# A linear-attention and two-FFN kernel whose later eight head pairs project q and k from raw float32 values on 64-row halves

## The chip, the cores and the metric

The kernel runs on one core of a Trainium2 chip. The metric is the device time of one execution in microseconds. Before the change it is 931.89 us, the median of three runs (930.95 to 933.46).

The engines are TensorE (PE, with its weight loads shown as PEld), VectorE (DVE), ScalarE (ACT), GpSimd (POOL) and SyncE (SP, which issues most transfers).

## The reference

Attention over 4 batches of 8 heads, 576 positions, 64 values each, then two FFNs over the 2304 tokens. The change lies in phi, the first lines:

```python
def phi(x):
    proj = np.einsum('bhsd,df->bhsf', x, w_phi)            # 64 -> 128 features
    proj = proj - np.max(np.abs(proj), axis=-1, keepdims=True)
    return np.concatenate([np.exp(proj), np.exp(-proj)], axis=-1)
q_p, k_p = phi(q), phi(k)
kv = np.einsum('bhsf,bhsd->bhfd', k_p, v)
z = np.sum(k_p, axis=2)
num = np.einsum('bhsf,bhfd->bhsd', q_p, kv)
den = np.einsum('bhsf,bhf->bhs', q_p, z)[..., None] + 1e-06
attn = num / den
# tokens x 512:
h = x @ w_in;  x = np.maximum(0.01 * h, h) @ w_out         # first FFN, 2048 wide
h = x @ w_in2; out = (h / (1 + np.exp(-h))) @ w_out2       # second FFN
```

## The kernel before

**Pairs.** The 32 heads are worked on in 16 pairs. A pair's q and k lie transposed in SBUF, head 0 in rows 0 to 63 and head 1 in rows 64 to 127. So a projection has a contraction of 64 per head. k has 576 positions: four chunks of 128, and a tail of 64 per head that is packed into one product.

**Two forms of a projection.** The first eight pairs (`NFULL = 8`) multiply raw float32 values. Pairs 2 to 7 take `wraw`, phi's weights twice above each other, and give each head a product of its own on its 64 rows (`f_pk`, line 432, `f_pq`, line 462; the tail is `f_kt`, line 438). The later eight pairs work with a split: ACT copies a value into the float32r type (the high part), DVE subtracts to get the low part (`s_split`, lines 276 to 292), and PE multiplies the parts as float32r on all 128 rows. For k, `s_pk` has three products per chunk (high by high, low by high, high by low, lines 322 to 324) against a block-diagonal weight of 256 columns, so both heads come out of one product; two chunks share a PSUM bank. For q, `s_pq` puts high and low part of one head above each other in the 128 rows and has two products per head (lines 354 and 355). The tail has two (lines 335 and 336). The weights' own split, `WH`, `BDH` and `BDL`, is made once at the start (`split_consts`).

**After the projection** of a later pair: `k_sub` (lines 299 and 300, DVE) takes the largest magnitude and subtracts it, `k_exp` (308 and 309, ACT) makes both exponentials, `s_kv` the products with v (389, 394). For q, ACT copies the projection out of PSUM (357), POOL reduces it, `s_eq` makes the exponentials, `num_split` has twelve products per half of the positions (577) and two ACT copies per head (580, 581), and `s_fin` puts the result into the FFN's input. Each pair calls `s_pq` and `num_split` twice, for 288 positions each.

**What PE does between.** The later pairs run between the products of the first FFN: a step is twelve products into one bank (853) and twelve into four banks of the other tag (884). PSUM has eight banks: four under the tag `a`, shared by the projections, numerators and line 853, and four under `y`.

**What sets the order.** Up to a planned time of 150, tables (`ORDER`, `PLAN`, `SLOTS`, `EARLY`) give each step a time, and `in_order` and `pin` hold each engine to that order. The later pairs are placed by offsets (`OFF1`, one pair per eight units) among the FFN steps, and the framework's scheduler sets the order of the instructions on each engine from there, waiting for a PSUM bank or a buffer where it must.

Of the kernel before, what the change touches and what calls it, by code (L numbers as in the profile page):

```python
# [8 lines left out]
F32 = mybir.dt.float32  # L9
F32R = mybir.dt.float32r  # L10
U32 = mybir.dt.uint32
AF = mybir.ActivationFunctionType
# [90 lines left out]
EARLY = {  # L103
    (8, "lq"): (117.29,),
    (8, "lv"): (117.39,),
    (8, "sp"): (123.8, 127.98, 131.89, 133.51, 137.47, 140.31, 142.48, 147.66),
    (9, "lq"): (151.8,),
    (8, "pq0"): (161.92, 162.63),
    (8, "eq0"): (165.65, 167.79, 171.38, 172.55, 173.81),
# [12 lines left out]
def tile_linear_attention_ffn_ffn(ctx: ExitStack, tc: tile.TileContext, q, k, v, w_phi, w_in1, w_out1, w_in2, w_out2, out):  # L122


    nc = tc.nc
    B, H, S, D = 4, 8, 576, 64
    F = (w_phi.shape[1] - 128) // 3
# [5 lines left out]
    S0 = 512  # L133
# [3 lines left out]
    NFULL = 8  # L137
# [12 lines left out]
    attc = att_ctx.enter_context(tc.tile_pool(name="attc", bufs=1))  # L150
# [4 lines left out]
    def at(shape, dt, tag):  # L155
        return att_pool[0].tile(shape, dt, tag=tag, bufs=AB[0].get(tag, 1), name=tag)

    def ps(tag):

        return psp.tile([128, 512], F32, tag=tag, name=f"ps_{tag}")  # L160
# [3 lines left out]
    ring, WIDE = [0], 2  # L164
# [45 lines left out]
                last[ins.engine] = ins  # L210
        return last

    wc = at([128, 3 * F + 128], F32, "wc")
    BDF, wraw, ident = wc[:, 0 : 2 * F].rearrange("p (j f) -> p j f", j=2), wc[:, 2 * F : 3 * F], wc[:, 3 * F :]
    WH = attc.tile([128, F], F32R, name="WH")
    BDH = attc.tile([128, 2, F], F32R, name="BDH")
    BDL = attc.tile([128, 2, F], F32R, name="BDL")

    def make_consts():
        for c in (slice(0, 2 * F), slice(2 * F, 3 * F + 128)):  # L220
# [1 line left out]
        first = [const.tile([128, 2], F32, name=f"first{i}") for i in range(2)]  # L222
        nc.gpsimd.memset(first[0], 0.0)
        nc.gpsimd.partition_all_reduce(first[1], first[0], 128, bass_isa.ReduceOp.absmax)

    def split_consts():
        nc.scalar.activation(WH, wraw, AF.Copy)
        nc.scalar.activation(BDH, BDF, AF.Copy)
        nc.vector.tensor_sub(BDL, BDF, BDH.bitcast(F32))


    tiles1 = [(462 * i, 462) for i in range(2)] + [(924 + 460 * i, 460) for i in range(3)]
    X1 = {}
# [16 lines left out]
    P = [dict() for _ in range(B * HP)]  # L250
# [19 lines left out]
    def sub(out_, x, h):  # L270
        return nc.vector.tensor_tensor(out_, x, h.bitcast(F32), op=ALU.subtract)  # L271
# [1 line left out]
    def full(i):  # L273
        return i < NFULL

    def s_split(i):

        st = P[i]
        h, l = at([128, S0], F32R, "krh"), at([128, S0], F32R, "krl")
        nc.scalar.activation(h, st["kr"], AF.Copy)  # L280
        sub(l, st["kr"], h)
        st["krh"], st["krl"] = h, l
        qs = at([128, 2, S], F32R, "qs")
        for j in range(2):
            r, o = (slice(0, 64), slice(64, 128))[:: 1 - 2 * j]
            nc.scalar.activation(qs[r, j], st["qr"][r], AF.Copy)
            sub(qs[o, j], st["qr"][r], qs[r, j])
        st["qs"] = qs
        t = at([128, 128], F32R, "kth")
        nc.scalar.activation(t, st["kt"], AF.Copy)  # L290
        sub(t[64:128], st["kt"][64:128], t[64:128])
        st["kth"] = t

    def k_sub(i, pk, ng, g0):

        ke = P[i]["ke"]
        km = at([128, 4], F32, "km")
        src = pk[:, 0 : ng * F].rearrange("p (g f) -> p g f", f=F)
        nc.vector.tensor_reduce(km[:, 0:ng], src, op=ALU.max, axis=AX.X, apply_absolute_value=True)
        nc.vector.tensor_tensor(  # L300
            ke[:, g0 : g0 + ng, 0, :], src, km[:, 0:ng].unsqueeze(2).to_broadcast([128, ng, F]), op=ALU.subtract
        )
# [5 lines left out]
        nc.scalar.activation(e1, e0, AF.Exp, scale=-1.0)  # L308
        nc.scalar.activation(e0, e0, AF.Exp)

    def s_pk(c2):
        def f(i):
            st = P[i]
            if c2 == 0:
                st["ke"] = at([128, 9, 2, F], F32, "ke")
            pk = ps("a")
            for u in range(2):
                c = 2 * c2 + u
                cs = slice(c * 128, (c + 1) * 128)
                o = pk[:, u * 2 * F : (u + 1) * 2 * F]  # L320
                bh, bl = BDH.rearrange("p j f -> p (j f)"), BDL.rearrange("p j f -> p (j f)")
                nc.tensor.matmul(o, st["krh"][:, cs], bh, start=True, stop=False)
                nc.tensor.matmul(o, st["krl"][:, cs], bh, start=False, stop=False)
                nc.tensor.matmul(o, st["krh"][:, cs], bl, start=False, stop=True)
            k_sub(i, pk, 4, 4 * c2)
            if c2 == 0:
                k_exp(i, 0, 4)

        return f

    def s_pkt(i):
        st = P[i]
        pk = ps("a")
        o = pk[:, 0:F]
        nc.tensor.matmul(o, st["kth"], WH, start=True, stop=False)
        nc.tensor.matmul(o, st["kth"], BDL[:, 0], start=False, stop=True)
        k_sub(i, pk, 1, 8)
        k_exp(i, 4, 9)

    def part(i, a):  # L340
# [3 lines left out]
    def s_pq(a):  # L344

        def f(i):
            st = P[i]
            c0, n = part(i, a)
            p = at([128, 2 * n], F32, "p")
            st["p", a] = p  # L350
            pq = [ps("a"), ps("a")]
            cs = slice(c0, c0 + n)
            for j in range(2):
                nc.tensor.matmul(pq[j][:, 0:n], WH, st["qs"][:, j, cs], start=True, stop=False)  # L354
                nc.tensor.matmul(pq[j][:, 0:n], BDL[:, j], st["qs"][:, j, cs], start=False, stop=True)  # L355
            for j in range(2):
                nc.scalar.activation(p[:, j * n : (j + 1) * n], pq[j][:, 0:n], AF.Copy)  # L357
            m = at([128, 2 * n], F32, "m")
            nc.gpsimd.partition_all_reduce(m, p, 128, bass_isa.ReduceOp.absmax)  # L359
            st["m", a] = m  # L360

        return f

    def s_eq(a):
        def f(i):
            st = P[i]
            c0, n = part(i, a)
            p, m = st["p", a], st["m", a]
            nc.vector.tensor_sub(m, p, m)
            qh = at([128, 2, 2 * n], F32R, "qh")  # L370
            st["qh", a] = qh
            ql = at([128, 2, 2 * n], F32R, "ql")
            st["ql", a] = ql
            for s in (1, 0):
                e = m if s == 0 else at([128, 2 * n], F32, "e")
                nc.scalar.activation(e, m, AF.Exp, scale=(1.0, -1.0)[s])
                nc.scalar.activation(qh[:, s], e, AF.Copy)
                sub(ql[:, s], e, qh[:, s])

        return f  # L380

    def kv_sign(i, s):
        st = P[i]
        ke, va = st["ke"], st["va"]
        if s == 1:
            st["kv"] = bank()
        pv = st["kv"][:, 0 : 4 * NKV].rearrange("p (s j d) -> p s j d", s=2, j=2)
        vf = va.rearrange("p c d -> p (c d)")
        nc.tensor.matmul(pv[:, s, :, 0 : D + 1], ke[:, 8, s, :], va[:, 8:10], start=True, stop=False, skip_group_check=True)  # L389
        for j in range(2):  # L390
            for c in range(4):
                w = (4 * j + c) * (D + 1)
                g = 4 * j + c if WIDE <= i < NFULL else 2 * c + j
                nc.tensor.matmul(  # L394
                    pv[:, s, j], ke[:, g, s, :], vf[:, w : w + NKV], start=False, stop=(j == 1 and c == 3), skip_group_check=True
                )
        return pv
# [22 lines left out]
    def f_pk(i):  # L420

        st = P[i]
        st["pk"] = [bank(), bank()]
        for c in range(4):
            if i < WIDE:
                o = st["pk"][c // 2][:, (c % 2) * 2 * F : (c % 2 + 1) * 2 * F]
                nc.tensor.matmul(o, st["kr"][:, c * 128 : (c + 1) * 128], wc[:, 0 : 2 * F], start=True, stop=True)
                continue
            for j in range(2):
                r = slice(64 * j, 64 * j + 64)  # L430
                o = st["pk"][j][:, c * F : (c + 1) * F]
                nc.tensor.matmul(o, st["kr"][r, c * 128 : (c + 1) * 128], wraw[r], start=True, stop=True)

    def f_kt(i):

        st = P[i]
        st["pk"].append(bank())
        nc.tensor.matmul(st["pk"][2][:, 0:F], st["kt"], BDF[:, 0], start=True, stop=True)
# [153 lines left out]
    def s_fin(a):  # L592
# [8 lines left out]

    W = 8.0
    fns = dict(
        lq=load_qk, lv=load_v, sp=s_split, pq0=s_pq(0), pq1=s_pq(1), pk0=s_pk(0), pk1=s_pk(1), pkt=s_pkt, eq0=s_eq(0), eq1=s_eq(1),
        kv=s_kv, num0=lambda i: num_split(i, 0), num1=lambda i: num_split(i, 1), fin0=s_fin(0), fin1=s_fin(1),
    )
    head = dict(
# [4 lines left out]
        for n_, f in dict(fpq=f_pq, fpc=f_pc, fpr=f_pr, fms=f_ms, fqx=f_qx, fn=f_n, fnd=f_nd, fnt=f_nt, ffx=f_fx).items():  # L612
            head[f"{n_}{a}"] = f(a)
    FIN = 16
    OFF1 = dict(lv=0.6, lq=-2.1250, sp=0.5, pq0=2.1172, pk0=4.0606, pk1=4.0616, pq1=4.7479, eq0=6.2094, pkt=5.1, kv=8.3898, num0=12.1423, eq1=13.9119, num1=14.457, fin0=FIN, fin1=FIN + 2.3)
    seq = [(t, i, n_) for n_, ts in ORDER.items() for i, t in enumerate(ts)]
    T0 = END - 2 * len(SLOTS)
    TL = T0 + 21.15 - min(OFF1.values())
# [587 lines left out]

    make_consts()
    wake()
    split_consts()
    run_att(END - 1e-3)  # L1210
    pin()

# [194 lines left out]
```

## Time and profile before

| | |
|---|---|
| median of three runs | 931.89 us |
| the profiled execution's own time | 932.26 us |
| its span, first to last instruction | 930.5 us |
| PE busy | 924.0 us, 99% of the span |
| DVE busy | 692.8 us, 74% |
| ACT busy | 615.9 us, 66% |
| mean granted TensorE clock | 0.999 |

The busy time of an engine is the time in which at least one of its instructions is on record. A matmul's record reaches over the start of the next, since they are pipelined; the pace is the distance between starts. A float32 product has two records, one for each of its two instructions, a float32r product has one. The idle time in front of an instruction is put down to what released it.

### The profile page before, as it was taken

What the parts mean: (1) busy time and instruction counts of PE and PEld (TensorE: products, weight loads), DVE (VectorE), ACT (ScalarE), POOL (GpSimd) and SP (SyncE); (2) the same over time, 40 slices, a digit from 0 to 9 for tenths busy, and PEclk for the clock granted to TensorE, in tenths of its full rate; (3) what the DMA queues carried; (4) which work ended last, traced back from release to release, by engine and by line L of the source; (5) the groups of instructions that cost most, each with busy time, mean ns of one, the idle gap of its engine ahead of it and who ended that gap; (6) DMA issues with size and microseconds to landing.
All of it is one profiled execution on the core that took longest, in us unless ns stands there. A gap on an engine that the chain in (4) does not pass through costs nothing.

```text
span 930.5 us, 15810 instructions
## 1 busy us (share of the span) xinstructions
PE 924.0 (99%) x5382; PEld 874.2 (94%) x5382; DVE 692.8 (74%) x1393; ACT 615.9 (66%) x1272; POOL 111.8 (12%) x110
## 2 busy tenths in 40 slices
PE   9999999999999999999999999999999999999998
PEld 7999988999999999998888899999999999999998
DVE  6989999967776665699898988888755377553753
ACT  6888787878777776466667757766645456454563
POOL 4343000111121120001111111111000000000000
PEclk9999999999999999999999999999999999999999
DMA  6755474473434642578877899999898778987784
GB/s 230 262 191 182 137 243 169 150 229 109 123 109 139 194 120 67 170 273 322 302 253 270 298 357 370 394 348 355 287 355 276 223 238 293 311 266 226 243 271 164
DMA packets 99647, 221.40 MB, mean 238 GB/s; under 512 B 14896, under 2 KB 25264, under 8 KB 99568
## 3 DMA queue, kind: packets, MB, share of 16 engines
q1 hardware_dynamic: 90496, 187.79, 60.7%
q0 software_dynamic: 8640, 32.25, 8.9%
q8 instruction: 43, 0.70, 0.3%
q10 hardware_dynamic: 432, 0.36, 0.1%
q14 instruction: 36, 0.29, 0.1%
HBM read 173.10 MB, written 47.22 MB: 237 GB/s over the span
## 4 chain that ended last, share of the span: by engine, by line
PE 97%; ACT 2%; DVE 1%; issue 0%; POOL 0%; ACTq 0%; DVEq 0%
PE ps_y L1165 19%; PE ps_y L884 17%; PE ps_a L853 13%; PE ps_y L1082 10%; PE ps_a L1082 10%; PE ps_a L993 8%; PE ps_a L394 5%; PE ps_a L884 4%; PE ps_a L577 3%; PE ps_a L525 2%; PE ps_y L394 1%; PE ps_y L525 1%; PE ps_a L389 1%; PE ps_a L354 0%; PE ps_a L355 0%; PE ps_a L462 0%
## 5 line engine op out<-in xcount | busy, mean ns | idle before, releaser
L1165 PE MATMUL ps_y<-gt,ws 128*128 128x384 f32 x1008 | 178.2, 337 | 0.0
L1165 PEld LDWEIGHTS ps_y<-gt,ws 128*128 128x128 f32 x1008 | 176.3, 188 | 1.0 <-DVE gt L271 0.7
L853 PE MATMUL ps_a<-xh,wi 128*128 128x462 f32 (+1 forms) x384 | 119.7, 374 | 0.6 <-ACT x L581 0.6
L884 PE MATMUL ps_y<-gh,wo 128*128 128x462 f32 (+1 forms) x440 | 102.4, 371 | 0.0
L1082 PE MATMUL ps_y<-xs,ws 128*128 128x384 f32 x504 | 98.1, 338 | 0.0
L1082 PE MATMUL ps_a<-xs,ws 128*128 128x384 f32 x504 | 96.5, 338 | 0.0
L703 ACT ACTIVATE gt<-g 128x384 fp32r<-128x384 f32 x120 | 62.2, 523 | 46.2 <-PE ps_y L1165 44.7
L884 PEld LDWEIGHTS ps_y<-gh,wo 128*128 128x128 f32 x440 | 81.9, 188 | 8.9
L1082 PEld LDWEIGHTS ps_y<-xs,ws 128*128 128x128 f32 x504 | 89.5, 188 | 0.3
L1082 PEld LDWEIGHTS ps_a<-xs,ws 128*128 128x128 f32 x504 | 89.3, 188 | 0.0
L271 DVE TENSOR_TENSOR gt<-g,gt 128x384 fp32r<-128x384 f32 x120 | 65.2, 557 | 31.8 <-ACT gt L703 31.4
L853 PEld LDWEIGHTS ps_a<-xh,wi 128*128 128x128 f32 x384 | 72.1, 188 | 8.8 <-ACT x L581 1.1
L853 PE MATMUL ps_a<-xl,wi 128*128 128x462 f32 (+1 forms) x192 | 71.4, 372 | 0.0
L1057 DVE TENSOR_TENSOR g<-ps_a,hs 128x384 f32<-128x384 f32 x36 | 20.0, 557 | 59.7 <-PE ps_a L1082 59.5
L359 POOL PARTITION_ALL_REDUCE m<-p x16 | 36.8, 2298 | 228.5 <-ACT p L357 176.0
L733 POOL DMA_DIRECT2D w7s<-wst x60 | 32.9, 549 | 231.9 <-DVE wst L271 190.3
L884 PE MATMUL ps_y<-gl,wo 128*128 128x462 f32 (+1 forms) x220 | 56.5, 374 | 0.0
L271 DVE TENSOR_TENSOR gl<-g,gh 128x462 fp32r<-128x462 f32 (+1 forms) x64 | 40.8, 637 | 10.3 <-ACT gh L864 8.1
L1053 ACT ACTIVATE hs<-ps_y 128x384 f32<-128x384 f32 x54 | 26.3, 487 | 33.5 <-DVE g L1057 31.5
L394 PE MATMUL ps_a<-va,ke 128*128 128x128 f32 x384 | 46.9, 275 | 0.0
L689 DVE CUSTOM_DVE_ANT_0 r<-t,r 128x1024 uint16<-128x1024 uint16 x64 | 45.4, 715 | 1.0
L884 PEld LDWEIGHTS ps_y<-gl,wo 128*128 128x128 f32 x220 | 41.3, 188 | 4.7
(215 smaller groups left out, 1967.2 us busy)
## 6 DMA issues: line engine op xcount, KB each, us to landing
ws<-w7s SPq DMA_DIRECT2D x336, 256.0 KB, 4.5
wo<-wos SPq DMA_DIRECT2D x46, 512.0 KB, 4.5
w7s<-wst POOLq DMA_DIRECT2D x45, 512.0 KB, 5.7
raw<-in_moe_w_out_dram SPq DMA_DIRECT2D x32, 512.0 KB, 5.0
rawi<-in_moe_w_in_dram SPq DMA_DIRECT2D x16, 512.0 KB, 5.9
wos<-wo SPq DMA_DIRECT2D x16, 512.0 KB, 2.9
raw<-in_moe_w_in_dram SPq DMA_DIRECT2D x16, 512.0 KB, 5.1
va<-in_v_dram SPq DMA_DIRECT2D x16, 325.0 KB, 5.2
```

The costliest lines, as they stand in the source:

```text
L271: return nc.vector.tensor_tensor(out_, x, h.bitcast(F32), op=ALU.subtract)
L359: nc.gpsimd.partition_all_reduce(m, p, 128, bass_isa.ReduceOp.absmax)
L394: nc.tensor.matmul(pv[:, s, j], ke[:, g, s, :], vf[:, w : w + NKV], start=False, stop=(j == 1 and c == 3), skip_group_check=True)
L525: nc.tensor.matmul(pb[:, w : w + NNUM], e[:, s, cs], KV[:, s, j], start=(s == 0), stop=(s == 1))
L689: nc.vector.tensor_tensor(r, t.bitcast(U32), r, op=ALU.add)
L703: nc.scalar.activation(h, f, AF.Copy)
L733: (nc.sync if seq else nc.gpsimd).dma_start(w7s[m_, p, :, i : i + m], o.bitcast(F32))
L853: nc.tensor.matmul(ph, a[:, kk, :], b_[:, kk, :], start=(m == 0), stop=(m == 3 * KD - 1))
L884: nc.tensor.matmul(Y[t][d][:, 0:n], a[:, ds_], b_, start=(c == 0 and m == 0), stop=(c == NC - 1 and m == 1), skip_group_check=True)
L993: nc.tensor.matmul(bank[b_], w1_of(p, wi_, a, kk), x1_of(xi, c, kk), start=(first and m == 0), stop=(m == 5), skip_group_check=True)
L1082: nc.tensor.matmul(bank[b_], w[:, a, kk], x[:, c, kk], start=(first and m == 0), stop=(m == 5), skip_group_check=True)
L1165: nc.tensor.matmul(bank[b_][db], w[:, a, db], t[:, c], start=(first and p_ == 0 and m == 0), stop=(p_ == NP - 1 and m == 2), skip_group_ch ...
```

## The change

The later eight pairs project as pairs 2 to 7 do. `s_split`, its due times and the split of phi's weights go. `s_pk(0)` calls `f_pk`, which makes all eight k products into two banks, one per head; `s_pk(1)` only subtracts for the second bank. `s_pkt` calls `f_kt`. `s_pq` has one product per head on 64 rows. The groups of `ke` are then ordered by head, as line 393 takes them. `wc`, the raw weights, moves into a pool that lives through the later pairs.

```diff
-    (8, "sp"): (123.8, 127.98, 131.89, 133.51, 137.47, 140.31, 142.48, 147.66),
...
-    wc = at([128, 3 * F + 128], F32, "wc")
+    wc = attc.tile([128, 3 * F + 128], F32, name="wc")
...
-    WH = attc.tile([128, F], F32R, name="WH")
-    BDH = attc.tile([128, 2, F], F32R, name="BDH")
-    BDL = attc.tile([128, 2, F], F32R, name="BDL")
...
-    def split_consts():
-        nc.scalar.activation(WH, wraw, AF.Copy)
-        nc.scalar.activation(BDH, BDF, AF.Copy)
-        nc.vector.tensor_sub(BDL, BDF, BDH.bitcast(F32))
...
-    def s_split(i):
-
-        st = P[i]
-        h, l = at([128, S0], F32R, "krh"), at([128, S0], F32R, "krl")
-        nc.scalar.activation(h, st["kr"], AF.Copy)
-        sub(l, st["kr"], h)
-        st["krh"], st["krl"] = h, l
-        qs = at([128, 2, S], F32R, "qs")
-        for j in range(2):
-            r, o = (slice(0, 64), slice(64, 128))[:: 1 - 2 * j]
-            nc.scalar.activation(qs[r, j], st["qr"][r], AF.Copy)
-            sub(qs[o, j], st["qr"][r], qs[r, j])
-        st["qs"] = qs
-        t = at([128, 128], F32R, "kth")
-        nc.scalar.activation(t, st["kt"], AF.Copy)
-        sub(t[64:128], st["kt"][64:128], t[64:128])
-        st["kth"] = t
...
-    def s_pk(c2):
+    def s_pk(j):
+
         def f(i):
             st = P[i]
-            if c2 == 0:
+            if j == 0:
                 st["ke"] = at([128, 9, 2, F], F32, "ke")
-            pk = ps("a")
-            for u in range(2):
-                c = 2 * c2 + u
-                cs = slice(c * 128, (c + 1) * 128)
-                o = pk[:, u * 2 * F : (u + 1) * 2 * F]
-                bh, bl = BDH.rearrange("p j f -> p (j f)"), BDL.rearrange("p j f -> p (j f)")
-                nc.tensor.matmul(o, st["krh"][:, cs], bh, start=True, stop=False)
-                nc.tensor.matmul(o, st["krl"][:, cs], bh, start=False, stop=False)
-                nc.tensor.matmul(o, st["krh"][:, cs], bl, start=False, stop=True)
-            k_sub(i, pk, 4, 4 * c2)
-            if c2 == 0:
+                f_pk(i)
+            k_sub(i, st["pk"][j], 4, 4 * j)
+            if j == 0:
                 k_exp(i, 0, 4)
 
         return f
 
     def s_pkt(i):
-        st = P[i]
-        pk = ps("a")
-        o = pk[:, 0:F]
-        nc.tensor.matmul(o, st["kth"], WH, start=True, stop=False)
-        nc.tensor.matmul(o, st["kth"], BDL[:, 0], start=False, stop=True)
-        k_sub(i, pk, 1, 8)
+        f_kt(i)
+        k_sub(i, P[i]["pk"][2], 1, 8)
         k_exp(i, 4, 9)
...
             for j in range(2):
-                nc.tensor.matmul(pq[j][:, 0:n], WH, st["qs"][:, j, cs], start=True, stop=False)
-                nc.tensor.matmul(pq[j][:, 0:n], BDL[:, j], st["qs"][:, j, cs], start=False, stop=True)
+                r = slice(64 * j, 64 * j + 64)
+                nc.tensor.matmul(pq[j][:, 0:n], wraw[r], st["qr"][r, c0 : c0 + n], start=True, stop=True)
...
-                g = 4 * j + c if WIDE <= i < NFULL else 2 * c + j
+                g = 4 * j + c if WIDE <= i else 2 * c + j
...
-    split_consts()
```

The changed file is shorter, so its lines have other numbers: 315 is the query product (354 and 355 before), 392 the k product and 398 the tail's (432 and 438 before), 537 the numerators (577), 813 and 844 the first FFN's products (853 and 884), and on ACT 280 and 336 exponentials (308 and 376), 376 the copy into the FFN's input (416), 540 and 541 the copies out of the numerators (580 and 581).

On PE, the end of pair 11's k products and what follows, before the change (four triples of lines 322 to 324 stand there):

```order
L322 MATMUL ps_a<-BDH,krh 128x256
L323 MATMUL ps_a<-BDH,krl 128x256
L324 MATMUL ps_a<-BDL,krh 128x256
L577 MATMUL ps_a<-qh,KVH 128x288
L577 MATMUL ps_a<-ql,KVH 128x288
L577 MATMUL ps_a<-qh,KVL 128x288
```

The same place in the changed kernel:

```order
L844 MATMUL ps_y<-gl,wo_2613 128x462 x4
L392 MATMUL ps_a<-wc,kr 128x128 x8
L537 MATMUL ps_a<-qh,KVH 128x288
L537 MATMUL ps_a<-ql,KVH 128x288
L537 MATMUL ps_a<-qh,KVL 128x288
```

Twelve products on 128 rows have become eight on 64 rows, and they stand between the FFN's products and the numerators as before.

On PE, the end of pair 8's second query call, before the change:

```order
L884 MATMUL ps_y<-gh,wo_1917 128x462 x4
L884 MATMUL ps_y<-gl,wo_1917 128x462 x4
L354 MATMUL ps_a<-qs,WH 128x288
L355 MATMUL ps_a<-qs,BDL 128x288
L884 MATMUL ps_y<-gh,wo_1975 128x462 x4
```

The whole of the same call in the changed kernel:

```order
L813 MATMUL ps_a<-xh,wi 128x462
L315 MATMUL ps_a<-qr,wc 128x288
L844 MATMUL ps_y<-gh,wo_1955 128x462 x4
L844 MATMUL ps_y<-gl,wo_1955 128x462 x4
L844 MATMUL ps_y<-gh,wo_1983 128x462 x4
L315 MATMUL ps_a<-qr,wc 128x288
```

The two heads' products stand apart here, as the two heads' couples did; in most calls the changed kernel has them in one row, `L315 MATMUL ps_a<-qr,wc 128x288 x2`.

On ACT, around the copies out of pair 10's first numerators, before the change (`krh` is the next pair's k):

```order
L416 ACTIVATE xh<-x 128x288
L376 ACTIVATE e<-m 128x576
L280 ACTIVATE krh<-kr 128x512
L376 ACTIVATE m<-m 128x576
L580 ACTIVATE d<-ps_a 1x288
L581 ACTIVATE x<-ps_a 64x288
L308 ACTIVATE ke<-ke 128x4x128
```

The same place in the changed kernel:

```order
L376 ACTIVATE xh<-x 128x288
L336 ACTIVATE e<-m 128x576
L336 ACTIVATE m<-m 128x576
L540 ACTIVATE d<-ps_a 1x288
L541 ACTIVATE x<-ps_a 64x288
L280 ACTIVATE ke<-ke 128x4x128
```

The conversion of k is gone, and the other instructions keep their order.

## Rows read from the trace of the kernel before

**Rows 1.** The page's first part: busy time, share of the span, instructions.

```profile
PE 924.0 (99%) x5382; PEld 874.2 (94%) x5382; DVE 692.8 (74%) x1393; ACT 615.9 (66%) x1272; POOL 111.8 (12%) x110
```

**Rows 2.** The page's chain that ended last, by engine.

```profile
PE 97%; ACT 2%; DVE 1%; issue 0%; POOL 0%; ACTq 0%; DVEq 0%
```

**Rows 3.** PE's waits, 150 to 360 us: total, times, longest.

```profile
PE ps_a L853 <- ACT x L581: 0.6, 2, 0.3
```

**Rows 4.** Timeline of PE, 238 to 266 us: start, duration, engine, line, operation.

```profile
240.36 0.28 PE L322 MATMUL ps_a<-BDH,krh 128*128 128x256 f32 x1
...
241.77 0.29 PE L577 MATMUL ps_a<-qh,KVH 128*128 128x288 f32 x1
...
246.26 0.30 PE L355 MATMUL ps_a<-qs,BDL 128*128 128x288 f32 x1
246.87 0.48 PE L853 MATMUL ps_a<-xh,wi 128*128 128x462 f32 x1 [0.31 <-ACT x L581]
247.19 0.38 PE L853 MATMUL ps_a<-xl,wi 128*128 128x462 f32 x1
...
249.52 0.23 PE L335 MATMUL ps_a<-WH,kth 128*128 128x128 f32 x1
...
249.69 0.35 PE L577 MATMUL ps_a<-qh,KVH 128*128 128x288 f32 x1
...
260.45 0.29 PE L354 MATMUL ps_a<-qs,WH 128*128 128x288 f32 x1
...
260.98 0.38 PE L853 MATMUL ps_a<-xh,wi 128*128 128x462 f32 x1
```

**Rows 5.** PE's instructions by line and shape: count, busy us, mean ns.

```profile
L354 PE MATMUL ps_a<-qs,WH 128*128 128x288 f32 x32 | 9.2, 302 | 0.0
...
L322 PE MATMUL ps_a<-BDH,krh 128*128 128x256 f32 x32 | 9.0, 280 | 0.0
```

**Rows 6.** Timeline of PE, 40 to 43 us.

```profile
40.35 0.48 PE L462 MATMUL ps_y<-qr,wc 64*128 64x256 f32 x1
40.36 0.48 PE L462 MATMUL ps_a<-qr,wc 64*128 64x256 f32 x1
40.67 0.38 PE L462 MATMUL ps_y<-qr,wc 64*128 64x256 f32 x1
...
41.43 0.27 PE L432 MATMUL ps_a<-wc,kr 64*128 64x128 f32 x1
...
42.21 0.27 PE L432 MATMUL ps_a<-wc,kr 64*128 64x128 f32 x1
...
42.42 0.49 PE L438 MATMUL ps_y<-wc,kt 128*128 128x128 f32 x2
42.74 0.50 PE L525 MATMUL ps_y<-KV,qh 128*128 128x128 f32 x3
```

**Rows 7.** Timeline of PE, 21.3 to 23 us.

```profile
21.46 0.61 PE L529 MATMUL ps_y<-KV,qh 128*128 128x130 f32 x4
22.00 1.16 PE L432 MATMUL ps_y<-wc,kr 64*128 64x128 f32 x16
```

**Rows 8.** Timeline of PE, 101 to 102.6 us.

```profile
101.74 0.47 PE L853 MATMUL ps_a<-xh,wi 128*128 128x462 f32 x1
102.05 0.37 PE L853 MATMUL ps_a<-xl,wi 128*128 128x462 f32 x1
102.26 0.58 PE L853 MATMUL ps_a<-xh,wi 128*128 128x462 f32 x2
```

**Rows 9.** Timeline of ACT, 238 to 262 us.

```profile
243.53 0.62 ACT L280 ACTIVATE krh<-kr 128x512 fp32r<-128x512 f32 x1
...
246.41 0.41 ACT L581 ACTIVATE x<-ps_a 64x288 f32<-64x288 f32 x1
```

**Rows 10.** Timeline of DVE, 238 to 262 us.

```profile
243.19 0.68 DVE L299 TENSOR_REDUCE km<-ps_a 128x4 f32<-128x512 f32 x1
243.91 0.69 DVE L300 TENSOR_TENSOR ke<-ps_a,km 128x512 f32<-128x512 f32 x1
```

More of the change, by code (lines that the diff above doesn't have):

```diff
@@ L351, in f @@
             pq = [ps("a"), ps("a")]
-            cs = slice(c0, c0 + n)
             for j in range(2):
-                nc.tensor.matmul(pq[j][:, 0:n], WH, st["qs"][:, j, cs], start=True, stop=False)
-                nc.tensor.matmul(pq[j][:, 0:n], BDL[:, j], st["qs"][:, j, cs], start=False, stop=True)
+                r = slice(64 * j, 64 * j + 64)
+                nc.tensor.matmul(pq[j][:, 0:n], wraw[r], st["qr"][r, c0 : c0 + n], start=True, stop=True)
             for j in range(2):
@@ L603, in tile_linear_attention_ffn_ffn @@
     fns = dict(
-        lq=load_qk, lv=load_v, sp=s_split, pq0=s_pq(0), pq1=s_pq(1), pk0=s_pk(0), pk1=s_pk(1), pkt=s_pkt, eq0=s_eq(0), eq1=s_eq(1),
+        lq=load_qk, lv=load_v, pq0=s_pq(0), pq1=s_pq(1), pk0=s_pk(0), pk1=s_pk(1), pkt=s_pkt, eq0=s_eq(0), eq1=s_eq(1),
         kv=s_kv, num0=lambda i: num_split(i, 0), num1=lambda i: num_split(i, 1), fin0=s_fin(0), fin1=s_fin(1),
@@ L614, in tile_linear_attention_ffn_ffn @@
     FIN = 16
-    OFF1 = dict(lv=0.6, lq=-2.1250, sp=0.5, pq0=2.1172, pk0=4.0606, pk1=4.0616, pq1=4.7479, eq0=6.2094, pkt=5.1, kv=8.3898, num0=12.1423, eq1=13.9119, num1=14.457, fin0=FIN, fin1=FIN + 2.3)
+    OFF1 = dict(lv=0.6, lq=-2.1250, pq0=2.1172, pk0=4.0606, pk1=4.0616, pq1=4.7479, eq0=6.2094, pkt=5.1, kv=8.3898, num0=12.1423, eq1=13.9119, num1=14.457, fin0=FIN, fin1=FIN + 2.3)
     seq = [(t, i, n_) for n_, ts in ORDER.items() for i, t in enumerate(ts)]
```

## The prediction, made before the changed kernel ran

> **What bounds the kernel now.** The page's first part comes first: PE is busy for 99% of the span, DVE for 74%, ACT for 66% [rows 1]. The chain that ended last says the same of the end: 97% of it is PE's own work [rows 2]. Since shares are averages, I then asked for PE's waits in the stretch from 150 to 360 us, where the later eight pairs run between the products of the first FFN. The answer is one line: two waits for the ScalarE copy of line 581 [rows 3]. So PE runs there almost without a gap. A microsecond of PE work added in that stretch comes out at the end, and work taken from ACT or DVE is worth only what it does to those two waits. What is left to do is to count PE time. Matmul records overlap (a record of 0.28 us is followed by the next after 0.12), so I count from start to start and call that distance a slot.
>
> **What PE loses.** In pair 11 the twelve k products run from 240.36 to 241.77: 1.41 us. A query call (four products of 288 columns) runs from 260.45 to 260.98: 0.53. The tail's two products run from 249.52 to 249.69: 0.17 [rows 4]. The counts (32 each of lines 322 and 354 [rows 5], the other lines by the code) are those of eight pairs: 8 x 1.41 + 16 x 0.53 + 8 x 0.17 = 21.1 us.
>
> **What PE gets.** The first pairs run these products in the new form. A raw float32 product is two instructions, each a slot, and the two 64-row halves run side by side: the query products into bank y and bank a start at 40.35 and 40.36 [rows 6]. The k group's eight slots start from 41.43 to 42.21, so a slot is 0.111 and the group 0.89 us. From 40.67 to 41.43 stand one slot of 256 and two of 320 columns, 896 columns in 0.76 us; 288 columns take 0.244, and a call, two slots, 0.49. The tail's product takes two slots, 0.22 (worked out in the next part). The order of the changed kernel has both halves of a query call next to each other in 14 calls; in two (pair 8's second, pair 10's first) other work stands between them, so that each half runs alone: four products of 0.49. Sum: 8 x 0.89 + 14 x 0.49 + 4 x 0.49 + 8 x 0.22 = 17.7 us, 3.4 less than before.
>
> **What a change of row height costs.** This is the term that turns the sign. In the first pairs 64-row products stand in a row of their kind, and full-height float32 products follow.
> - Going in: four instructions of line 529 start at 21.46; at 0.11 each they end at 21.90, but the next group, 64 rows, starts at 22.00 [rows 7]: 0.10. That group's record lasts 1.16 us, while the k group that follows other 64-row work lasts from 41.43 to 42.21 + 0.27 = 42.48, 1.05 [rows 6]: 0.11 more, its first slot is twice as long.
> - Going out: the last 64-row slot ends at 42.32, the next product starts at 42.42: 0.10. The two slots of that product end at 42.74, 0.32 after, of which 0.22 is streaming: 0.10 again. Out of the transposes' 64-row products into the FFN's first product the first slot is 0.31 (101.74 to 102.05) and the next 0.21 [rows 8], the same 0.10 where a float32r product follows.
>
> So a group of 64-row products between full-height ones pays 0.2 on each side, 0.4 in all. The Trainium skill names this: "Changing tiling mode (not just tile) drains the TensorE" (TensorEngine Tiling (Array Packing), Key Properties); the trace agrees, with 0.2 for each change. The page puts no figure to it; another (TensorE: Matmul & The Clock Gate, Single matmul latency) gives some 166 ns as what a lone warm product can't hide behind a neighbour, and by that, an estimate, the 50 changes below would cost 8.3 us instead of 10.0 and the sum would be 1.7 lower. The rows decide.
>
> The changed kernel's order has 25 such groups in the stretch: 8 of k, 14 whole query calls, 4 halves, less one because pair 9's first call stands directly before its k group. 25 x 0.4 = 10.0 us. No row shows the way in from a float32r product, so I bound that side by 0 and 0.3 (a gain is excluded, since the slots themselves are counted already) and take 0.2, the float32 row. By these numbers a query call goes from 0.53 to 0.89, a k group from 1.41 to 1.29. PE in all: -3.4 + 10.0 = +6.6 us.
>
> **What goes with ACT's and DVE's splits.** In pairs 10 and 11 PE stands still after the second query call: line 355 starts at 246.26 and line 853 at 246.87 instead of 0.13 later, and its first slot is 0.32 instead of 0.21 [rows 4]: 0.59 each, 1.2 us for the two waits. It waits for the bank that the last copy of line 581 reads, 246.41 to 246.82. On ACT the conversion of the next pair's k, 0.62 us at 243.53, stands before that copy [rows 9], and it goes; PE also arrives some 0.2 us later. Both waits should vanish: -1.2.
>
> What is late next is PSUM. The k group now takes two banks at once, and DVE frees each with a reduce and a subtract, 1.3 us for one bank (243.19 to 244.60) [rows 10]. In a usual pair some 4 us of numerators and FFN products stand between the k group and the next need of a bank, and DVE loses a 0.6 us subtract there, so I cost it at nothing. Without that cover it is up to 2.6 us. In pair 9 only the twelve numerators (1.6 us) stand between the k group and the second query call. There I add 0.5, between 0 and 2.5.
>
> The other edits cost nothing. The conversion of phi's weights is off PE's path, since its first products read the raw weights. The loads are as many as before, and the two buffers of raw k and q are now held until the products, whereas the next load into one belongs to two pairs on. The subtract of bank 1 of pair 8's k stands by its due time before that of bank 0, which both wait for the same group.
>
> Sum: 6.6 - 1.2 + 0.5 = +5.9 us. The profiled execution took 932.26 us (span 930.5), 0.37 above the median of 931.89. So 938.2 on its own scale, 937.7 as a median.
>
> **Rivals.**
> - *The height change is hidden.* PE loads the next weights behind the running products, whatever their height, and only the halving counts: -3.4 - 1.2 = -4.6, 927.3 us, faster. The sign turns where a group costs less than some 0.17. For it: the two halves do run side by side. The Trainium skill's "Up to 2×" for a contraction of 64 (TensorEngine Tiling (Array Packing), Theoretical Speedup) reads this way. Against it: each height change in rows 6 to 8 pays, the one before an FFN product too. 4%.
> - *Only the way out costs.* The way in from a float32r product is free: 25 x 0.2 = 5.0, and -3.4 + 5.0 - 1.2 + 0.5 = +0.9, 932.8. For it: no row shows this way in. Against it: the drain is one of the array, and the rows show it alike on both sides. 10%.
> - *Banks become the bound.* If in each of the eight pairs the second query call or the FFN product behind it waits 0.5 us or more for DVE's subtract, with the halves of the call then running one after the other, 4 to 8 us come on top: 942 to 946. For it: the waits of pairs 10 and 11 are of this kind. Against it: both engines lose work just there. 8%.
>
> **How the numbers follow.** The forecast has 78%, with its own range from 935 to 940. About 0.3%, 2.8 us, is what a measurement of this kernel can tell from no change, so "slower" is above 934.7. The forecast and the banks lie there but for a small part, 85%; the second rival is within the bound, 11%; the first is faster, 4%. For eight times in ten I go from 933.6, where the way in costs 0.03 a side, to 941, where it costs 0.3 and PSUM waits add another microsecond.
>
> **What would show it.** Right: the products of k and q in the changed kernel's timeline start as pairs 0.01 us apart; a query call between FFN products takes about 0.9 us from its first start to the next FFN start plus that product's longer first slot; the k group 1.2 to 1.3; PE's busy time grows by some 6 us, while DVE and ACT lose work. The wait for line 581's copy is gone from PE's waits. Wrong: halves that start one after the other (then a call costs 1.4 and the kernel is past 945), a first slot of 0.24 where a 64-row group begins (then the second rival), or new lines in PE's waits with more than 1 us behind DVE's subtract of line 300.

## The result, and the profile after

The changed kernel takes 937.84 us, the median of four runs (937.59 to 938.30). The kernel before takes 931.63 in its four (930.95 to 933.46). The ratio is 1.0067, with a 95% interval from 1.0055 to 1.008: slower by 6.2 us, as forecast (937.7).

The first part of the page of the changed kernel, and its chain that ended last, answer to [rows 1] and [rows 2]:

```profile
PE 929.6 (99%) x5414; PEld 866.0 (93%) x5414; DVE 666.7 (71%) x1360; ACT 600.3 (64%) x1238; POOL 109.5 (12%) x110
```

```profile
PE 97%; ACT 1%; DVE 1%; DMA 0%; POOL 0%; SPq 0%; issue 0%; DVEq 0%; ACTq 0%
```

DVE is relieved of 26 us and ACT of 16, and no more of that reaches the end than the two waits of [rows 3]. PE gains 5.6 us of busy time and is still 97% of the chain. The mean granted clock is 1.000, against 0.999 before, so the clock is not behind the loss.

PE's waits over the whole execution of the changed kernel (waiting line, what it waited for: total, times, longest) are four. All of them lie outside the later pairs: the same stretch, 150 to 360 us, that had one line in [rows 3] has none now.

```profile
PE ps_y L1165 <- DVE z L1163: 1.2, 1, 1.2
PE ps_y L398 <- ACT p L433: 0.8, 1, 0.8
PE ps_a L422 <- DMA qr<-in_q_dram: 0.3, 1, 0.3
PE ps_a L485 <- ACT KV L472: 0.2, 1, 0.2
```

So the time can't be in waits that this view names. It is in the distances between starts. The timeline of PE in the changed kernel, pair 11 (start, duration, operation; to be laid beside [rows 4]):

```profile
243.18 1.00 PE L844 MATMUL ps_y<-gl,wo 128*128 128x462 f32 x4
244.10 1.16 PE L392 MATMUL ps_a<-wc,kr 64*128 64x128 f32 x16
245.19 0.40 PE L537 MATMUL ps_a<-qh,KVH 128*128 128x288 f32 x1
245.43 0.29 PE L537 MATMUL ps_a<-ql,KVH 128*128 128x288 f32 x1
245.56 0.30 PE L537 MATMUL ps_a<-qh,KVL 128*128 128x288 f32 x1
...
248.57 1.01 PE L844 MATMUL ps_y<-gl,wo 128*128 128x462 f32 x4
249.51 0.76 PE L315 MATMUL ps_a<-qr,wc 64*128 64x288 f32 x4
250.20 0.48 PE L813 MATMUL ps_a<-xh,wi 128*128 128x462 f32 x1
250.51 0.38 PE L813 MATMUL ps_a<-xl,wi 128*128 128x462 f32 x1
250.73 0.58 PE L813 MATMUL ps_a<-xh,wi 128*128 128x462 f32 x2
```

Read a query call from it. Line 844's four products should take 4 x 0.21 = 0.84; from 248.57 to 249.51 are 0.94, so 0.10 goes before the 64-row products start. From 249.51 to 250.20 are 0.69, and the two slots that run side by side stream for 0.49: 0.20 more (the single records show where: the first slot lasts 0.34 instead of 0.24, and 0.10 passes after the last). The first FFN product then has 0.31 to the next start, where the slot after it has 0.22: 0.10 again. In all 0.49 + 0.40 = 0.89 us, where [rows 4] have 0.53 before. The k group the same way: 0.92 for line 844's four products (+0.08), 1.09 for eight slots of 0.111 (+0.20), 0.24 for a numerator that has 0.13 (+0.11): 1.29, before 1.41.

Line 581's copy of before, which held up pairs 10 and 11, is line 541 now, and line 813 starts 0.68 and 0.69 behind the second call's first start in these pairs, which is the call's own length.

**Where the 6.2 us are.** From the first product of the first FFN to the first of the second, PE's starts span 321.48 us before (84.57 to 406.05) and 328.00 after (83.72 to 411.72): +6.5. The head in front of it was 0.86 shorter in this execution and the rest behind it 0.36, so that the span grew by 5.3 only. That the head is the change's doing is not shown: in the six other kernels below it ends between 83.71 and 84.53. The shortest of these still makes the weights' split, and two whose edits to the changed kernel lie behind the head (the third and the fourth experiment) have 84.33 and 84.16.

I measured the 25 groups of 64-row products one by one: from the last start in front to the second start behind, less the slots. 23 of them cost 0.39 to 0.41 us, the four halves that stand alone among them: two halves side by side are not what costs. The two of pair 9 cost 0.95 and 1.15. The timelines of pair 9, PE's products, PE's weight load, and ACT:

```profile
191.52 1.01 PE L844 MATMUL ps_y<-gl,wo 128*128 128x462 f32 x4
192.46 0.76 PE L315 MATMUL ps_a<-qr,wc 64*128 64x288 f32 x4
193.05 1.60 PE L392 MATMUL ps_a<-wc,kr 64*128 64x128 f32 x16
194.58 0.40 PE L537 MATMUL ps_a<-qh,KVH 128*128 128x288 f32 x1
...
196.37 1.51 PE L315 MATMUL ps_a<-qr,wc 64*128 64x288 f32 x4
197.81 0.48 PE L813 MATMUL ps_a<-xh,wi 128*128 128x462 f32 x1
```

```profile
197.13 0.29 PEld L315 LDWEIGHTS ps_a<-qr,wc 64*128 64x128 f32 x2 [0.46 <-ACT x L541]
```

```profile
196.67 0.40 ACT L541 ACTIVATE x<-ps_a 64x288 f32<-64x288 f32 x1
```

The second query call's record lasts 1.51 instead of 0.76: its halves run one after the other. The second half's weights are loaded at 197.13, when ACT's copy of the numerators has given up a bank at 197.07. PE was not idle on record while it waited, since the first half still ran; only the weight load's row shows the wait. The k group lasts 1.60 instead of 1.16, and by its single records its second half starts 0.45 behind its first; what that half waited for no row names, and it stays open.

### The profile page after: what moved, and what is told of

Same layout as the page of the kernel before. It is cut to its first block, busy times and chain, and to the rows that moved or that the text cites. A ratio compares the mean times of both kernels' runs of the same rounds, so it can differ in the third digit from the quotient of the medians.

```text
span 935.8 us, 15797 instructions
## 1 busy us (share of the span) xinstructions
PE 929.6 (99%) x5414; PEld 866.0 (93%) x5414; DVE 666.7 (71%) x1360; ACT 600.3 (64%) x1238; POOL 109.5 (12%) x110
## 4 chain that ended last, share of the span: by engine, by line
PE 97%; ACT 1%; DVE 1%; DMA 0%; POOL 0%; SPq 0%; issue 0%; DVEq 0%; ACTq 0%
PE ps_y L1125 19%; PE ps_y L844 17%; PE ps_a L813 13%; PE ps_y L1042 9%; PE ps_a L1042 9%; PE ps_a L953 7%; PE ps_a L354 5%; PE ps_a L844 4%; PE ps_a L537 3%; PE ps_a L485 2%; PE ps_a L315 1%; PE ps_a L392 1%; PE ps_y L354 1%; PE ps_y L485 1%; PE ps_a L349 1%; DMA qr<-in_q_dram 0%
## 5 line engine op out<-in xcount | busy, mean ns | idle before, releaser
L319 POOL PARTITION_ALL_REDUCE m<-p x16 | 34.6, 2161 | 237.0 <-ACT p L317 152.7
L819 ACT ACTIVATE g<-ps_a 128x462 f32<-128x462 f32 (+1 forms) x48 | 26.6, 554 | 30.6 <-PE ps_a L813 30.4
```

## The experiments

All of them are read by the same stretch between the two FFNs' first products ("the stretch": 321.48 before, 328.00 after), and by the ratio to runs of the kernel before on the same chip.

**Only k's products, the tail with them.** The kernel before, with q still split:

```diff
     def s_split(i):
-        h, l = at([128, S0], F32R, "krh"), at([128, S0], F32R, "krl")
...
-                nc.tensor.matmul(o, st["krh"][:, cs], bh, start=True, stop=False)
-                nc.tensor.matmul(o, st["krl"][:, cs], bh, start=False, stop=False)
-                nc.tensor.matmul(o, st["krh"][:, cs], bl, start=False, stop=True)
+            if c2 == 0:
+                f_pk(i)
...
     def s_pkt(i):
-        nc.tensor.matmul(o, st["kth"], WH, start=True, stop=False)
-        nc.tensor.matmul(o, st["kth"], BDL[:, 0], start=False, stop=True)
+        f_kt(i)
```

> k and its tail raw as in the changed kernel, q split as before (phi's weights split again for it). Theory (a change of row height costs 0.2 us each way): twelve k products of 1.41 us a pair become a group of 0.89 + 0.4; pair 8's group is broken into three here, so ten groups: -11.3 + 7.1 + 0.2 + 10 x 0.4 + 0.4 for the tail = +0.4, and the two waits of 0.59 go with the conversion of k on ACT: -0.8 in all, 0.999 of the kernel before, some 930.9 us. Rival (the changed kernel's cost is the query products' alone, k gets its halving for nothing): -4.2 + 0.4 - 1.2 = -5.0, some 926.6 us.

Measured: 933.31 us (932.62 to 935.61), ratio 1.0027, from 1.0017 to 1.0037. Neither theory gave a loss. The groups are as predicted (nine of ten cost 0.38 to 0.41, pair 9's 0.95), so the height's price stands; what failed is my sum of the waits. The profiled execution is the slowest of the eight, 935.61, 2.3 above the median. PE's waits in the stretch, and behind it:

```profile
PE ps_a L974 <- DVE g L960: 0.8, 1, 0.8
...
PE ps_a L834 <- DVE ke L292: 0.5, 1, 0.5
PE ps_a L335 <- ACT x L562: 0.4, 1, 0.4
PE ps_a L834 <- ACT g L840: 0.4, 1, 0.4
PE ps_y L865 <- ACT gh L684: 0.3, 1, 0.3
```

and the timeline of PE at two of the three places in the stretch:

```profile
196.62 0.29 PE L336 MATMUL ps_a<-qs,BDL 128*128 128x288 f32 x1
197.33 0.40 PE L335 MATMUL ps_a<-qs,WH 128*128 128x288 f32 x1 [0.42 <-ACT x L562]
...
201.98 0.29 PE L558 MATMUL ps_a<-qh,KVL 128*128 128x288 f32 x1
202.75 0.45 PE L834 MATMUL ps_a<-xh,wi 128*128 128x462 f32 x1 [0.47 <-DVE ke L292]
```

A slot that should last 0.13 lasts 0.71 and 0.77. The stretch is 323.04, +1.56, and that nearly adds up: the products -3.8 (8 x 1.41 + 8 x 0.17 before, 8 x 0.89 + 8 x 0.22 after), two products of pair 8 that run alone +0.2, ten groups +4.0, pair 9's bank +0.55, the two waits of before -1.2, three new ones +1.9 by their slots; +1.7, within 0.2. In place of the waits of pairs 10 and 11 there are others. Behind the stretch this profile has 522.60 us to PE's last end, where all the other kernels have 520.4 to 520.9; the first and the last wait above lie there. Why they do, these runs do not show.

**Only q's products.** k and its tail split as before:

```diff
-        qs = at([128, 2, S], F32R, "qs")
...
-                nc.tensor.matmul(pq[j][:, 0:n], WH, st["qs"][:, j, cs], start=True, stop=False)
-                nc.tensor.matmul(pq[j][:, 0:n], BDL[:, j], st["qs"][:, j, cs], start=False, stop=True)
+                r = slice(64 * j, 64 * j + 64)
+                nc.tensor.matmul(pq[j][:, 0:n], wraw[r], st["qr"][r, c0 : c0 + n], start=True, stop=True)
```

> q raw on 64 rows as in the changed kernel, k and its tail split as before. Theory: 15 whole calls and 2 halves, 17 x 0.49 against 16 x 0.53, and 17 groups x 0.4 = 6.8: +6.6 on PE; the two waits shrink from 0.59 to some 0.25, since PE arrives later but ACT still converts k: -0.7. +5.9, some 937.5 us, nearly all of the change's loss. Rival (the loss is in PSUM waits behind the k group's two banks): no loss here, 931 us or less.

Measured: 937.42 us (937.15 to 938.80), ratio 1.0071, from 1.0058 to 1.0085; the stretch +6.22. Nearly the whole loss is q's, and the rival (no loss) is out. The parts do not simply add: in the stretch q alone costs 6.2, k alone 1.6, both together 6.5. The sum: 17 groups x 0.4 = +6.8, products -0.15 (15 calls of 0.49 and one in halves, 0.98, against 16 x 0.53), pair 9's second call +0.74, the two waits -1.2; +6.2. One wait is left in PE's list for the stretch; it is that of pair 9's second call, already in the sum:

```profile
PE ps_a L847 <- ACT x L575: 0.5, 1, 0.5
```

ACT still converts k here (0.63 us, ahead of the copies as in [rows 9]), and yet the waits of pairs 10 and 11 are gone. So the removal of k's conversion is not needed for it. Whether they go because PE comes later this run alone does not tell, since q's conversions, which are ACT's too, are gone here; the part on the prediction reads it from the copies.

**q's products raw, but on all 128 rows.** The changed kernel, with phi's weights block-diagonal and zeros against the other head:

```diff
-                r = slice(64 * j, 64 * j + 64)
-                nc.tensor.matmul(pq[j][:, 0:n], wraw[r], st["qr"][r, c0 : c0 + n], start=True, stop=True)
+                nc.tensor.matmul(pq[j][:, 0:n], BDF[:, j], st["qr"][:, c0 : c0 + n], start=True, stop=True)
```

> The changed kernel, but each query product takes raw float32 q on all 128 rows against the block-diagonal weights (zeros in the other head's rows), so its height is that of its neighbours. Theory (the height is the price): a call is four slots of 0.244, 0.98 us, with no longer first slot; only the eight k groups pay 0.4. Against the kernel before: -1.0 for k, +0.4 tail, +7.1 for q, -1.2 waits = +5.3, some 937.0 us; first slots of query calls and of the products behind them as long as the others. Rival (the price is the change from float32r to raw float32, whatever the height): 0.4 per call on top, +6.4, some 943.5 us, and the long first slots stay.

Measured: 938.61 us (937.64 to 939.41), ratio 1.0079, from 1.0066 to 1.0091. The rival was that the change of type (float32r to float32) costs, whatever the height. The timeline of PE shows no such price:

```profile
248.52 1.01 PE L843 MATMUL ps_y<-gl,wo 128*128 128x462 f32 x4
249.37 1.13 PE L314 MATMUL ps_a<-qr,wc 128*128 128x288 f32 x4
250.12 0.59 PE L812 MATMUL ps_a<-xh,wi 128*128 128x462 f32 x1
250.55 0.37 PE L812 MATMUL ps_a<-xl,wi 128*128 128x462 f32 x1
```

Line 843's four products take their 0.85: nothing drains in front. From 249.37 to 250.55 are 1.18 us, which is four slots of 0.242 and one FFN slot of 0.21. (The call and the product behind it have to be read together: by the single records that product is already started 0.03 behind the start of the fourth query slot, so that its own 0.43 to the next start holds most of that slot.) The call costs 0.97 and nothing around it. It too takes two banks, at the same place in the order, and in the changed kernel the gap in front is 0.09 to 0.10 in all 25 groups, so that is no wait for a bank either. So the price belongs to the row height. It also shows how little the halves win: 0.89 on 64 rows against 0.97 on 128, and less than nothing in the two calls whose halves stand apart (2 x 0.89). Over all calls it is 16 x 0.97 = 15.5 here and 18 x 0.89 - 0.4 = 15.6 in the changed kernel, where one call stands directly before a k group: as good as equal. The median is 0.8 above the changed kernel's, the stretch 0.4 (328.41); the two intervals overlap. My own theory here is low all the same: +5.3 was put, and the stretch has +6.9. It left out pair 9, whose k group costs 0.95 here too, and where PE's list has two waits that the changed kernel's has not (0.2 in the second query call for ACT's copy, 0.3 behind the next numerators for DVE's subtract).

**k's products in two groups.** The changed kernel, with the first two chunks in step `pk0` and the other two in `pk1`, placed later, so that full-height products come between:

```diff
             if j == 0:
-                f_pk(i)
-            k_sub(i, st["pk"][j], 4, 4 * j)
+                f_pk(i, range(2))
+                return
+            f_pk(i, range(2, 4))
+            k_sub(i, st["pk"][0], 4, 0)
...
-    OFF1 = dict(lv=0.6, lq=-2.1250, pq0=2.1172, pk0=4.0606, pk1=4.0616, pq1=4.7479, eq0=6.2094, pkt=5.1, kv=8.3898, num0=12.1423, eq1=13.9119, num1=14.457, fin0=FIN, fin1=FIN + 2.3)
+    OFF1 = dict(lv=0.6, lq=-2.1250, pq0=2.1172, pk0=4.0606, pk1=4.1430, pq1=4.7479, eq0=6.2094, pkt=5.1, kv=8.3898, num0=12.1423, eq1=13.9119, num1=14.457, fin0=FIN, fin1=FIN + 2.3)
```

> The changed kernel, but the k products are made in two groups of four, one before and one behind the numerators, in most pairs: the same products, 32 groups of 64 rows instead of 25. Theory: 7 x 0.4 = 2.8 us more than the changed kernel, some 940.6 us, with no new waits of PE. Rival (a price per product or per microsecond, not per group): as the changed kernel, 937.8 us.

Measured: 941.82 us (941.33 to 942.04), ratio 1.0113, from 1.0099 to 1.0127, 4.0 above the changed kernel. The products are the same in number and kind; the groups are 32 instead of 25. PE's timeline, pair 11:

```profile
243.80 0.99 PE L847 MATMUL ps_y<-gl,wo 128*128 128x462 f32 x4
244.73 0.72 PE L395 MATMUL ps_a<-wc,kr 64*128 64x128 f32 x8
245.37 0.40 PE L540 MATMUL ps_a<-qh,KVH 128*128 128x288 f32 x1
245.61 0.29 PE L540 MATMUL ps_a<-ql,KVH 128*128 128x288 f32 x1
...
246.94 0.29 PE L540 MATMUL ps_a<-qh,KVL 128*128 128x288 f32 x1
247.16 0.71 PE L395 MATMUL ps_a<-wc,kr 64*128 64x128 f32 x8
247.80 1.95 PE L847 MATMUL ps_y<-gh,wo 128*128 128x462 f32 x8
```

Each half group takes 0.64 from start to start, where four slots of 0.111 stream for 0.44, and delays both neighbours by 0.1. All groups outside pair 9 cost 0.39 to 0.41, whether 128 or 288 columns wide. The stretch is 331.28, 3.3 above the changed kernel's: 7 x 0.4 = 2.8, and a new wait of some 0.7 (line 816 for ACT, at 334), 0.2 more than the whole. The theory had no new wait. The remaining 0.7 of the medians' 4.0 lies outside the stretch or between executions. The price goes by group.

**Only k's chunks, the tail split.** As the first experiment, but `s_pkt` and the tail's split are left as before.

> The first experiment with the tail split as before, all eight pairs' other k products raw. Theory: -0.1 for k (ten groups), -1.2 for the two waits, plus what waits the scheduler's order brings: 930 without any, 933.5 with those of the first experiment (three of 0.6 among pairs 9 and 10, two behind the last pair). The trace's waits of PE tell which.

Measured: 932.34 us (931.84 to 933.42), ratio 1.0008, from 0.9999 to 1.0017. The stretch is +0.73; nine groups cost 0.39 to 0.41 and pair 9's 0.84. Its own sum (products -4.1, pair 9's with one that runs alone, ten groups +4.0, pair 9 +0.44, two waits gone -1.2, two new ones +1.1) gives +0.2, so 0.5 is not accounted for. PE's waits in the stretch are again new ones, at other places:

```profile
PE ps_a L343 <- ACT x L570: 0.4, 1, 0.4
PE ps_a L842 <- ACT g L848: 0.4, 1, 0.4
```

**Only k's chunks, in pairs 10 to 15.** This leaves out pairs 8 and 9, where the order cut the groups up (pair 8: three in the first experiment) or held a bank:

```diff
+    KRAW = 10
...
+        if i < KRAW:
+            h, l = at([128, S0], F32R, "krh"), at([128, S0], F32R, "krl")
...
+            if i >= KRAW:
+                if c2 == 0:
+                    f_pk(i)
+                pk = st["pk"][c2]
```

> The kernel before, with raw k products on 64-row halves in pairs 10 to 15 alone; their tail, all q and pairs 8 and 9 are split as before. Theory: six groups of 0.89 + 0.4 for 1.41, -0.7; the two waits of 0.59 (pairs 10 and 11) go with ACT's conversion of k, -1.2; no place with the banks of pair 9: -1.9, some 929.2 us, 0.998 of the kernel before. Rival (as in the first experiment, a changed order brings waits of its own, some 3 us): 932 or more.

Measured: 931.14 us (930.08 to 932.42) in eleven runs, against 931.53 in twenty-one of the kernel before; ratio 0.9998, from 0.999 to 1.0007. This is no measurable difference, and short of the expected gain. Its six groups cost 0.402 to 0.405 each, so that a k group is 0.12 cheaper than before, six times 0.7. One of the two waits of [rows 3] is gone, the other one is still there, now in pair 10 alone:

```profile
PE ps_a L862 <- ACT x L590: 0.4, 1, 0.4
```

In the profiled execution the stretch is 1.15 shorter than before, which is about these two; the medians do not resolve it. No version here beats the kernel before by what can be told.

## Why the prediction was right

**The price of the height change** was the term that turned the sign, and it is right in mechanism and size: 0.39 to 0.41 in 23 of 25 groups, where 25 x 0.4 = 10.0 was put. The way in from a float32r product, which no row of before showed and which I bounded by 0 and 0.3, costs the 0.2 that I took: 0.10 in front of the group, and 0.10 in its first slot. The rival that only the way out costs falls with it, and the rival that the change is hidden too. All of these runs agree with the Trainium skill's sentence on the drain (TensorEngine Tiling (Array Packing), Key Properties). The estimate of 8.3 us, worked out with the Trainium skill's 166 ns (TensorE: Matmul & The Clock Gate, Single matmul latency), is 1.7 too low against the rows; that page gives the figure as the constant part of the latency of a single bf16 product, and to take it for a change of height was my step. Nor was the Trainium skill's "Up to 2×" (TensorEngine Tiling (Array Packing), Theoretical Speedup) worth much here: the streaming of a call is halved, from 0.97 to 0.49, and the call with its surroundings goes from 0.97 to 0.89.

**The products** are right: 0.111 and 0.242 a slot, and the halves run side by side in all whole calls but that of pair 9. The tail's was worked out and not read before. The changed kernel's timeline of PE in pair 11:

```profile
252.62 0.37 PE L813 MATMUL ps_a<-xh,wi 128*128 128x462 f32 x1
252.83 0.38 PE L398 MATMUL ps_a<-wc,kt 128*128 128x128 f32 x2
252.97 0.38 PE L537 MATMUL ps_a<-qh,KVH 128*128 128x288 f32 x1
253.18 0.29 PE L537 MATMUL ps_a<-ql,KVH 128*128 128x288 f32 x1
```

From 252.83 to 253.18 are 0.35 us, less the numerator's own 0.13 it is the 0.22 of the sum.

**The waits of pairs 10 and 11** vanish, -1.2, as put, but the reasons given do not carry the whole of it. In pair 11, the last numerator on PE and the ACT copy that frees the bank, in the kernel before (its copy is in [rows 9]), in the changed kernel, with k alone and with q alone:

```profile
243.23 0.29 PE L577 MATMUL ps_a<-qh,KVL 128*128 128x288 f32 x1
...
246.76 0.30 PE L537 MATMUL ps_a<-qh,KVL 128*128 128x288 f32 x1
247.96 0.41 ACT L541 ACTIVATE x<-ps_a 64x288 f32<-64x288 f32 x1
...
245.82 0.30 PE L558 MATMUL ps_a<-qh,KVL 128*128 128x288 f32 x1
247.02 0.41 ACT L562 ACTIVATE x<-ps_a 64x288 f32<-64x288 f32 x1
...
245.98 0.29 PE L571 MATMUL ps_a<-qh,KVL 128*128 128x288 f32 x1
247.61 0.41 ACT L575 ACTIVATE x<-ps_a 64x288 f32<-64x288 f32 x1
```

From the start of that numerator the copy ended after 3.59 us before, and ends after 1.61, 1.61 and 2.04 in the others. PE wants the bank, for the FFN product behind the second query call, after 3.16 (246.26 + 0.13, the wait left out), 3.44, 3.19 and 3.41. So PE does come 0.3 later in the changed kernel (0.2 was put), but that alone would have left a wait; the copy comes 2.0 earlier, three times the 0.62 of the conversion. With k alone the wait is gone although PE comes no later. Nor does the conversion settle it: with q alone it is still there, and in the last experiment, without it, the copy of pair 10 stays late (3.73). What puts ACT's work ahead or behind in a pair these runs do not separate.

**Pair 9's bank** was mis-sized: +0.5 was put, and it is +1.3 (0.55 in the k group, 0.75 in the second call), within the bounds of 0 and 2.5. I had named DVE's subtract as the late reader. For the second call the record names ACT's copy of the numerators instead (DVE's subtract ends within 0.02 of it), and the size comes from the halves then running one after the other: 0.75 more, which I had priced in the rival on banks but not here. That rival itself did not come: in pairs 10 to 15 each whole call runs in halves side by side. One reading behind the bound was off: DVE's two rows for one bank reach over 1.41 us (243.19 to 244.60), not 1.3.

Added up with the measured terms, 6.6 - 1.2 + 1.3 = 6.7, and the stretch grew by 6.5. With the sum's 5.9 the median came out 0.1 from the forecast (5.9 on 931.89 is 937.8; 937.7 was put). That closeness is luck, since the terms were further off: 0.8 too little for pair 9, against differences of the same size in the head alone.

**What the sum could not have told** is the first experiment's lesson: with k alone the same counting missed by 2 us and more, because the scheduler's order then left other bank waits. In the full change pair 9 alone waits for a copy; from pair 10 on the copies of the numerators in front of a second call end 1.6 to 1.7 us behind the last of them, and PE wants the bank 3.4 behind it. Nothing in the sum said that the new order would leave no other waits. The forecast was also helped by that.

## What to carry to other kernels

In this kernel a group of 64-row products between full-height ones pays 0.4 us, however many products it has: count the groups in the order, not the products, and use the halves only where one group saves more than that. Putting such groups next to each other should share the price, as the first pairs' rows suggest; no run here tried it as a change of its own. On 128 rows with zeros the same product pays nothing around it, and the calls added up were within 0.1 us of the halves here. Where PE is busy for 99%, an edit that takes PE work away can bring bank waits at other places, as the two runs with k alone in all eight pairs had; so add up the waits of the new order before a gain below some 2 us is believed.

## What the runs showed of the hardware that was not expected

- The price is the same to within 0.02 us for groups of 4 instructions of 288 columns and of 8 or 16 of 128, and behind a float32 product (line 354, in front of one half of pair 10's first call) as behind float32r ones.
- Where one of the two banks was late (pair 9's second call), the 64-row halves ran one after the other, 1.51 against 0.76 us for the call. PE's own waits say nothing of it; the wait stands at the weight load (0.46).
- The start of the first FFN differs by 0.9 us between the eight profiles (83.71 to 84.57), one for each kernel, over kernels with and without the weights' split: a single profile's span is no measure for a change of that size.
